# Second MLP: product 3 behind product 2, an earlier activation split, other places for the input splits, and a last quarter turned by TensorE

## The chip, the cores and the metric

The kernel runs on one core of a Trainium2 chip. The metric is the device time of one execution in microseconds; the kernel before takes 965.82 us (median of 3 runs, 965.8 to 967.69). A smaller number is better.

## The reference

The reference chains three blocks in float32. Attention: 4 x 8 heads, 576 positions, 64 channels, with a causal mask and a forgetting bias. Then two MLPs over 2304 tokens of width 512 with 2048 hidden units:

```python
x = np.ascontiguousarray(attn_out.transpose(0, 2, 1, 3)).reshape(B * S, H * D)
h = x @ w_in;  g = np.maximum(h, 0.0) + alpha * np.minimum(h, 0.0);  x = g @ w_out     # first MLP
h = x @ w_in;  r = np.maximum(h, 0.0);  g = r * r;                   out = g @ w_out   # second MLP
```

The weights come as float64 and are converted on the chip.

## The kernel before

**Precision.** A float32 operand is split into a rounded part and the rest (`split2`: ScalarE copies into the rounded type, VectorE subtracts, L927 and L928). A matmul of two such operands takes three terms (`TERMS`).

**Order.** Attention comes first, then the first MLP, then the second. The first MLP runs 48 steps: 3 passes of 768 tokens by 16 blocks of hidden units. A step is 24 matmuls into two `ph` banks (L601), the activation on VectorE (`gg`, L621 and L622), its split `gs` (L624, L625), and 24 matmuls into `po` (L887) for the step before. Beside it, weights are converted from float64 (`conv`: two ScalarE, two VectorE and one GpSimd instruction; L120 to L129). `convert(step, behind)` takes from the list `todo` what is due at that step, and `issue_after(behind)` puts it behind a given instruction on that instruction's engine. At steps 3 to 11 two conversions are due at each; they are all written ahead of the step's matmuls.

**Second MLP.** It uses a seven-product scheme (Strassen's, in Winograd's form) on halves: for each of 3 passes of 768 tokens, stage 1 makes the hidden activations and stage 2 the output.

- Stage 1 loops over 8 blocks q. Each has seven products of 6 matmuls of 384 columns (L1012), into four PSUM banks: a (products 1 and 2), b (6 and 7), c (5 and 3), d (4). The order on TensorE is 1, 6, 5 of block q, then product 3 of block q-1 (`end(q - 1)`), then 2, 4, 7 of block q. ScalarE copies a to `p1` behind product 1 (L1031), before product 2 accumulates into a. Behind product 7, VectorE makes u3 = p1 + b (L1060) and c22 = u3 + c (L1061). c22 reads bank c, into which product 3 then accumulates; so product 3 of a block waits for c22 of that block. `end` then adds c to u2 (L1043), and ScalarE and GpSimd square the activation (L1022, L1023). For odd q VectorE also subtracts two slots of `g` (L1047).
- The weights of stage 1 arrive in groups of up to 512 columns (`w1f`) and are split into `w1h` by `split2`, fetched three groups ahead.
- Stage 2 has 28 items (i, q): seven products by four quarters, in `ORDER2`, each a block of 12 matmuls (L1144), first the six of output half m = 0, then the six of m = 1. Its operand `th` (3 buffers) is a split of `g`, written by `prepare` `AHEAD` = 2 items ahead; for products 6, 7 and 4 a subtraction of two slots of `g` comes first (L1095).
- In `fill(n)`, behind block n of stage 2, the eleven steps of the next pass's input split (`x_steps`: splits into `xc` and differences in `xl`) are spread over the blocks n in (2, 3, 4, 5, 6, 7, 13, 14, 24, 25, 26), each behind the latest `th` split on ScalarE and VectorE.
- At the end of an output quarter VectorE adds the accumulator to `k` (L1164) and turns it in 32 x 32 blocks (L1130), and four DMAs store it with 256-byte rows (`store`, L1108). The last quarter of the last pass ends the kernel.

**What sets the order.** In the second MLP `in_order` chains TensorE's instructions as written. On the other engines a planner sets the order: it lays the program out on simulated time and takes, among the instructions that are ready, the one written first. `chain` still holds the last TensorE instruction of the pass before when a pass starts.

Of the kernel before, what the change touches and what calls it, by code (L numbers as in the profile page):

```python
# [8 lines left out]
F32 = mybir.dt.float32  # L9
# [10 lines left out]
def attention_then_two_mlps(  # L20
# [13 lines left out]
    nc = tc.nc  # L34
    B, H, S, D = q.shape
    P = 128
# [964 lines left out]
    def stage1(stream, fill):  # L1001

        def product(i, q, pt, first, last):
            s = SLOT[i]
            hl = stream.need(q, s // 2)
            c0 = (s % 2) * 256
            cnt = 0
            for kb in range(2):  # L1010
                for a, b in TERMS:
                    nc.tensor.matmul(  # L1012
                        pt[:, :HT], hl[:, a, c0 + kb * P : c0 + (kb + 1) * P], xc[i][:, b, kb, :],
                        start=(first and cnt == 0), stop=(cnt == 5), skip_group_check=not first,
                    )
                    cnt += 1

        def t15(name):
            return pools["m2"].tile([P, HT], F32, name=name, tag=name, bufs=2)

        def act(dst, r, h):
            nc.scalar.activation(r, h, AF.Relu)  # L1022
            nc.gpsimd.tensor_tensor(dst, r, r, ALU.mult)  # L1023

        hold = {}

        def begin(q):
            a, b, c, d = bank("a"), bank("b"), bank("c"), bank("d")
            product(1, q, a, True, True)
            p1 = t15("p1")  # L1030
            nc.scalar.copy(p1, a[:, :HT])  # L1031
            product(6, q, b, True, True)
            u2 = t15("u2")
            nc.vector.tensor_add(u2, p1, b[:, :HT])
            if q % 2 == 0:
                g_t[q // 2] = pools["m2"].tile([P, 2, 4, HT], F32, name="g", tag="g", bufs=NQ // 2)
            g = g_t[q // 2][:, q % 2]
            hold[q] = a, b, c, d, p1, u2, g

        def end(q):  # L1040
            a, b, c, d, p1, u2, g = hold.pop(q)
            product(3, q, c, False, True)
            nc.vector.tensor_add(u2, u2, c[:, :HT])  # L1043
            act(g[:, 1, :], u2, u2)
            if q % 2:
                gq = g_t[q // 2]
                last_g[0] = ins_of(nc.vector.tensor_sub(gq[:, :, 1], gq[:, :, 1], gq[:, :, 0]))  # L1047

        for q in range(NQ):
            begin(q)  # L1050
            a, b, c, d, p1, u2, g = hold[q]
            product(5, q, c, True, True)
            if q > 0:
                end(q - 1)
            product(2, q, a, False, True)
            act(g[:, 0, :], g[:, 0, :], a[:, :HT])
            product(4, q, d, True, True)
            product(7, q, b, False, True)
            u3, c22 = t15("u3"), t15("c22")
            nc.vector.tensor_add(u3, p1, b[:, :HT])  # L1060
            nc.vector.tensor_add(c22, u3, c[:, :HT])  # L1061
            nc.vector.tensor_add(u3, u3, d[:, :HT])
            act(g[:, 3, :], c22, c22)
            act(g[:, 2, :], u3, u3)
            fill(NQ - 1 - q)
            in_order(IN_ORDER[:1])
        return lambda: end(NQ - 1)

    PLACE = {1: 0, 5: 1, 6: 1, 2: 2, 7: 0, 4: 2, 3: 3}
    ORDER2 = (1, 5, 6, 2, 7, 4, 3)  # L1070
    AHEAD = 2

    class Stage2:


        def __init__(self, p):
            self.p = p
            self.items = [(i, q) for i in ORDER2 for q in range(NQ // 2)]
            self.th, self.slab, self.done, self.subs = {}, {}, 0, []

# [20 lines left out]
        def store(self, mh, h, yt):  # L1101
            for u in range(4):
                cs = slice(mh * 256 + 64 * u, mh * 256 + 64 * (u + 1))
                src = yt[32 * u : 32 * (u + 1)].rearrange("r j c m -> r j (c m)")
                e = nc.scalar if (self.p, mh, h) == (1, 0, 1) and u % 2 else nc.sync
                if self.p < 2:
                    r0 = (2 * self.p + h) * S
                    e.dma_start(out[r0 : r0 + HT, cs].rearrange("(j r) c -> r j c", r=32), src)  # L1108
                    continue
                for z in range(2):  # L1110
                    r0 = (2 * h + z) * S + 3 * P
                    e.dma_start(
                        out[r0 : r0 + 3 * TAIL, cs].rearrange("(j r) c -> r j c", r=32), src[:, 6 * z : 6 * (z + 1)]
                    )

        def run(self, fill):
            kept = {}
# [11 lines left out]
            def turn(yt, src, m):  # L1129
                nc.vector.transpose(yt[:, :, :, m], src)  # L1130

            accs = {}
            for n, (i, q) in enumerate(self.items):
                self.prepare(n + AHEAD)

# [3 lines left out]
                acc = accs[j]  # L1139
                th = self.th.pop((i, q))  # L1140
                ws = self.slab[i, q // 2]
                for m, qq, z in [(m, qq, z) for m in range(2) for qq in range(2) for z in range(3)]:
                    x, y = TERMS[z]
                    nc.tensor.matmul(  # L1144
                        acc[m][:, :HT], ws[:, y, (2 * q + qq) % 4, m * P : (m + 1) * P], th[:, x, qq, :],
                        start=(i == j and q == 0 and qq == 0 and z == 0),
                        stop=(q == NQ // 2 - 1 and qq == 1 and z == 2), skip_group_check=True,
                    )
                fill(n)
                if q < NQ // 2 - 1:  # L1150
                    continue
# [25 lines left out]
    handed = 0  # L1177
    xl_now[0] = xT[0]

    def convert(step, behind):  # L1180
        while todo and todo[0][0] <= step:
            with tc.issue_after(behind):
                _, what, args = todo.pop(0)
                what(*args)
            if loads and what in (w_conv, prep_conv):
                w_load(*loads.pop(0))

    for step, (c, f) in enumerate(steps):
        wi_now = wi
        if step >= 3:  # L1190
            convert(step, anchor)
        if step > 0 and step + 1 < len(steps):
            wi = split_w(0, steps[step + 1][1], 0)
        if step >= 3:
# [13 lines left out]
        pend.append([c, f, gs, wo])  # L1208
        if len(pend) > 1:
            mlp_out(*pend.pop(0))  # L1210
        if step < 3:
            convert(step, last_gg[0])
            in_order((mybir.EngineType.DVE, mybir.EngineType.Activation))
# [23 lines left out]
    pools["m2"] = ctx.enter_context(tc.tile_pool(name="m2", bufs=1, reuse_waits="tile"))  # L1237
    pools["ps"] = ctx.enter_context(tc.tile_pool(name="ps", bufs=8, space=PSUM, reuse_waits="tile"))

    PASSES = (0, 2, 1)  # L1240
    for z, p in enumerate(PASSES):
        s2 = Stage2(p)

        def early(left):
            with tc.issue_after(last_w1[0]):
                if left < 4:
                    i, q = s2.items[2 * (3 - left)]
                    s2.fetch(i, q // 2)
                if left == NQ // 2 and z + 1 < NPASS:
                    load_x(PASSES[z + 1])  # L1250
            if left == 0:
                s2.prepare(AHEAD)

        chain["at"] = len(nc.cur_bb.bb.instructions)
        close = stage1(stream if z == 0 else Stream(), early)
        steps2 = x_steps() if z + 1 < NPASS else []

        def fill(n):
            if n == 1:
                close()  # L1260
            in_order(IN_ORDER[:1])
            if n in (2,3,4,5,6,7,13,14,24,25,26) and steps2:
                with tc.issue_after(s2.last[0]), tc.issue_after(s2.last[1]):
                    steps2.pop(0)()

# [32 lines left out]
```

## Time and profile before

| | |
|---|---|
| median of 3 runs | 965.82 us |
| profiled execution, own time | 965.55 us |
| its span, first to last instruction | 963.8 us |
| outside the span | 1.75 us |
| TensorE busy (matmuls) | 946.8 us, 98% |
| VectorE busy | 787.7 us, 82% |
| ScalarE busy | 552.0 us, 57% |
| GpSimd busy | 340.1 us, 35% |
| granted TensorE clock, mean | 0.996 |

The profile has several views. The page gives the busy time of each engine. The view by windows gives busy time and number of instructions of each engine in chosen stretches. The view of waits lists how long an engine sat idle and what ended the idle time. The timeline lists the instructions of a stretch in order of time, merged where one line repeats: start, duration, engine, line, operation, tiles (written <- read), shape, count, and in brackets idle time and what ended it. The view of one line or tile gives durations as least/median/most. PE is TensorE, DVE VectorE, ACT ScalarE, POOL GpSimd, SP SyncE; a q behind a name is that engine's queue issuing DMAs. A matmul's duration overlaps the next one's, so the distance between starts is its price.

### The profile page before, as it was taken

What the parts mean: (1) busy time and instruction counts of PE and PEld (TensorE: products, weight loads), DVE (VectorE), ACT (ScalarE), POOL (GpSimd) and SP (SyncE); (2) the same over time, 40 slices, a digit from 0 to 9 for tenths busy, and PEclk for the clock granted to TensorE, in tenths of its full rate; (3) what the DMA queues carried; (4) which work ended last, traced back from release to release, by engine and by line L of the source; (5) the groups of instructions that cost most, each with busy time, mean ns of one, the idle gap of its engine ahead of it and who ended that gap; (6) DMA issues with size and microseconds to landing.
All of it is one profiled execution on the core that took longest, in us unless ns stands there. A gap on an engine that the chain in (4) does not pass through costs nothing.

```text
span 963.8 us, 16690 instructions
## 1 busy us (share of the span) xinstructions
PE 946.8 (98%) x5951; PEld 891.3 (92%) x5951; DVE 787.7 (82%) x1423; ACT 552.0 (57%) x1146; POOL 340.1 (35%) x341
## 2 busy tenths in 40 slices
PE   8999999999999999999999999999999999999997
PEld 6888888898999999999999999999999999999997
DVE  7788878879888887778987868788987899878685
ACT  6899888846544543345644634566435664366432
POOL 7466554133333453453253410343004430044200
PEclk9999999999999999999999999999999999999999
DMA  5777765324444344434653632676756767547385
GB/s 142 197 201 200 185 163 130 85 92 135 131 131 132 109 159 142 142 127 159 214 173 120 197 120 74 198 273 204 254 150 182 279 193 260 140 128 268 121 257 127
DMA packets 121446, 161.33 MB, mean 167 GB/s; under 512 B 50546, under 2 KB 94706, under 8 KB 115986
## 3 DMA queue, kind: packets, MB, share of 16 engines
q1 hardware_dynamic: 120112, 159.69, 54.1%
q8 instruction: 47, 0.77, 0.3%
q10 hardware_dynamic: 1250, 0.57, 0.3%
q14 instruction: 37, 0.30, 0.1%
HBM read 121.85 MB, written 30.11 MB: 158 GB/s over the span
## 4 chain that ended last, share of the span: by engine, by line
PE 84%; DVE 8%; issue 2%; ACT 2%; DMA 2%; SPq 1%; POOL 0%; ACTq 0%; DVEq 0%; POOLq 0%
PE ph L601 18%; PE po L887 17%; PE acc L1144 15%; PE ps_tr L500 5%; PE c L1012 4%; PE a L1012 4%; PE b L1012 4%; PE ps_xb L550 3%; PE d L1012 2%; PE ps_xa L534 2%; PE ps_sc L392 2%; PE ps_sc L393 2%; PE ps_tr L321 2%; PE ps_sc L398 2%; DVE xc L928 1%
## 5 line engine op out<-in xcount | busy, mean ns | idle before, releaser
L601 PE MATMUL ph<-xs,wi_hi 128*128 128x384 f32 x768 | 195.7, 335 | 1.2 <-DVE gg L622 1.2
L1144 PE MATMUL acc<-th,w2s 128*128 128x384 f32 x1008 | 176.7, 335 | 0.5 <-DVE th L928 0.5
L1144 PEld LDWEIGHTS acc<-th,w2s 128*128 128x128 f32 x1008 | 174.8, 188 | 1.5 <-DVE th L928 1.5
L887 PE MATMUL po<-gs,wo_hi 128*128 128x256 f32 (+1 forms) x768 | 166.1, 336 | 0.0
L601 PEld LDWEIGHTS ph<-xs,wi_hi 128*128 128x128 f32 x768 | 136.0, 188 | 3.6 <-DVE gg L622 1.5
L887 PEld LDWEIGHTS po<-gs,wo_hi 128*128 128x128 f32 x768 | 121.3, 188 | 14.0
L601 PE MATMUL ph<-xs,wi_lo 128*128 128x384 f32 x384 | 128.3, 334 | 0.0
L927 ACT CAST th<-g 128x768 fp32r<-128x768 f32 x84 | 70.3, 837 | 74.7 <-PE acc L1144 61.1
L624 ACT CAST gs<-gg 128x768 fp32r<-128x768 f32 (+1 forms) x48 | 39.8, 829 | 113.3 <-DVE gg L622 113.2
L928 DVE TENSOR_TENSOR w1h<-w1f,w1h 128x512 fp32r<-128x512 f32 x96 | 79.1, 825 | 29.8 <-ACT w1h L927 29.7
L887 PE MATMUL po<-gs,wo_lo 128*128 128x256 f32 (+1 forms) x384 | 98.9, 335 | 0.0
L928 DVE TENSOR_TENSOR th<-g,th 128x768 fp32r<-128x768 f32 x84 | 83.2, 990 | 17.1 <-ACT th L927 16.6
L129 POOL TENSOR_TENSOR wf<-cv_t,wf 128x512 uint32<-128x512 uint32 x32 | 45.8, 1430 | 92.7 <-DVE cv_t L125 78.0
L129 POOL TENSOR_TENSOR wc<-cv_t,wc 128x512 uint32<-128x512 uint32 x24 | 39.4, 1646 | 104.6 <-DVE cv_t L125 52.4
L625 DVE TENSOR_TENSOR gs<-gg,gs 128x768 fp32r<-128x768 f32 (+1 forms) x48 | 46.6, 971 | 36.3 <-ACT gs L624 36.3
L1023 POOL TENSOR_TENSOR g<-g 128x384 f32<-128x384 f32 x24 | 19.9, 829 | 155.7 <-ACT g L1022 155.7
L621 DVE TENSOR_SCALAR gg<-ph,alpha_sb 128x384 f32<-128x384 f32 x95 | 58.0, 611 | 19.9 <-PE ph L601 19.9
L419 DVE CUSTOM_DVE_ANT_0 pr<-ps_sc,mask 128x128 f32<-128x128 f32 (+3 forms) x128 | 61.7, 486 | 15.1 <-PE ps_sc L393 12.1
L601 PEld LDWEIGHTS ph<-xs,wi_lo 128*128 128x128 f32 x384 | 72.0, 188 | 0.1
L927 ACT CAST w1h<-w1f 128x512 fp32r<-128x512 f32 x96 | 53.8, 564 | 31.8 <-PE b L1012 8.2
L432 ACT ACTIVATE pr<-pr,nmax 128x128 f32<-128x128 f32 (+3 forms) x128 | 71.2, 557 | 0.4
L887 PEld LDWEIGHTS po<-gs,wo_lo 128*128 128x128 f32 x384 | 59.3, 188 | 7.7
(167 smaller groups left out, 2022.9 us busy)
## 6 DMA issues: line engine op xcount, KB each, us to landing
w2s<-w2D SPq DMA_DIRECT2D x42, 1024.0 KB
w1f<-w1D SPq DMA_DIRECT2D x72, 256.0 KB
raw_w<-in_moe_w_in_dram SPq DMA_DIRECT2D x32, 512.0 KB
w2D<-whl SPq DMA_DIRECT2D x16, 896.0 KB
raw_w<-in_moe_w_out_dram SPq DMA_DIRECT2D x24, 512.0 KB
iv<-sD SPq DMA_DIRECT2D x32, 144.0 KB
raw_q<-in_q_dram SPq DMA_DIRECT2D x16, 256.0 KB
raw_v<-in_v_dram SPq DMA_DIRECT2D x32, 128.0 KB
```

Of the source, the lines that this page charges most:

```text
L129: nc.gpsimd.tensor_tensor(d, tt, d, ALU.add)
L419: nc.vector.tensor_tensor_reduce(o, banks.pop(("s", i, h))[:, :w], m, -1.0, first, ALU.add, ALU.min, nmax[:, h : h + 1])
L432: nc.scalar.activation(o, o, AF.Exp, bias=m, scale=-1.0, accum_out=sums_of[n][:, i, h : h + 1])
L500: last = nc.tensor.transpose(ps[:, z * P : (z + 1) * P], pr[:, c0 : c0 + P], ident)
L601: nc.tensor.matmul(ph[h][:, :HT], ws[a][:, kb * P : (kb + 1) * P], xs[kb][:, bb, h * HT : (h + 1) * HT], start=(cnt == 0), stop=(cnt == 3 ...
L621: nc.vector.tensor_scalar(x, ph[h][:, :HT], 0.0, alpha_sb[:, f : f + 1], ALU.min, ALU.mult)
L625: sub = nc.vector.tensor_sub(z[:, 1], a, z[:, 0].bitcast(F32))
L887: nc.tensor.matmul(acc, ws[a][:, m * P : (m + 1) * P], gs[:, bb, c_], start=first_ and z == 0, stop=lst and z == 2, skip_group_check=True,)
L927: a = nc.scalar.copy(dst[:, 0], src)
L928: v = nc.vector.tensor_sub(dst[:, 1], src, dst[:, 0].bitcast(F32))
L1012: nc.tensor.matmul(pt[:, :HT], hl[:, a, c0 + kb * P : c0 + (kb + 1) * P], xc[i][:, b, kb, :], start=(first and cnt == 0), stop=(cnt == 5), ...
L1144: nc.tensor.matmul(acc[m][:, :HT], ws[:, y, (2 * q + qq) % 4, m * P : (m + 1) * P], th[:, x, qq, :], start=(i == j and q == 0 and qq == 0 ...
```

## The change

Six edits, all but one in the second MLP:

1. In stage 1, product 2 and the activation of its result are written ahead of `end(q - 1)`, so product 3 of the block before follows product 2.
2. `AHEAD` is 3, and stage 2's first three `th` are prepared one block of stage 1 earlier (`left == 1`).
3. The input split of the next pass goes to the blocks (2, 3, 4, 5, 12, 13, 14, 24, 25, 26, 27).
4. `chain.clear()` at the start of a pass: TensorE's first instruction of a pass is no longer chained to the last one of the pass before.
5. In the last pass the last quarter of the output is done by `finish`. TensorE's order is block n (m = 0), block n-1 (m = 1), three turns of m = 0, block n (m = 1), three turns of m = 1. VectorE adds m = 1 in three parts of 128 columns, TensorE turns each against the identity into PSUM, ScalarE or VectorE copies it out, and three DMAs of 128 rows of 1 KB store it, two on SP's queue and one on ScalarE's.
6. In the first MLP at steps 3 to 11, one conversion is written ahead of the step and the rest behind `mlp_out`, with VectorE's part behind the step's `gg`.

```diff
             product(5, q, c, True, True)
+            product(2, q, a, False, True)
+            act(g[:, 0, :], g[:, 0, :], a[:, :HT])
             if q > 0:
                 end(q - 1)
-            product(2, q, a, False, True)
-            act(g[:, 0, :], g[:, 0, :], a[:, :HT])
             product(4, q, d, True, True)
...
-    AHEAD = 2
+    PASSES = (0, 2, 1)
+    AHEAD = 3
...
+        def finish(self, n, block, acc, k2):
+            y = pools["m2"].tile([P, 3, P, 2], F32, name="yt", tag="yt", bufs=2)
+            tp = [bank(f"t{tb}") for tb in range(3)]
+
+            def add(m, c):
+                nc.vector.tensor_add(k2[:, m, c], k2[:, m, c], acc[m][:, c])
+
+            def turn(m, tb):
+                nc.tensor.transpose(tp[tb][:, m * P : (m + 1) * P], k2[:, m, tb * P : (tb + 1) * P], ident)
+
+            def evac(m, tb, e):
+                (nc.scalar.copy if e else nc.vector.tensor_copy)(y[:, tb, :, m], tp[tb][:, m * P : (m + 1) * P])
+
+            block(n, 0)
+            add(0, slice(0, HT))
+            block(n - 1, 1)
+            for tb in range(3):
+                turn(0, tb)
+            for tb in range(3):
+                evac(0, tb, 1)
+            block(n, 1)
+            for tb in range(3):
+                add(1, slice(tb * P, (tb + 1) * P))
+            for tb in range(3):
+                turn(1, tb)
+                evac(1, tb, tb < 2)
+                r0 = (2 * self.p + 1) * S + tb * P
+                (nc.scalar if tb == 1 else nc.sync).dma_start(
+                    out[r0 : r0 + P, 0:256], y[:, tb].rearrange("p f m -> p (f m)")
+                )
+            in_order(IN_ORDER[:1])
...
-                for m, qq, z in [(m, qq, z) for m in range(2) for qq in range(2) for z in range(3)]:
+                if not self.final or n < len(self.items) - 2:
+                    block(n, 0)
+                    block(n, 1)
+                elif n < len(self.items) - 1:
+                    block(n, 0)
+                else:
+                    self.finish(n, block, acc, kept[2])
+                    return
...
-    def convert(step, behind):
-        while todo and todo[0][0] <= step:
+    def convert(step, behind, n=99):
+        while todo and todo[0][0] <= step and n > 0:
+            n -= 1
...
-            convert(step, anchor)
+            convert(step, anchor, 1 if step < 12 else 99)
...
             mlp_out(*pend.pop(0))
+        if 3 <= step < 12:
+            convert(step, last_gg[0])
...
-            if left == 0:
+            if left == 1:
                 s2.prepare(AHEAD)

+        chain.clear()
         chain["at"] = len(nc.cur_bb.bb.instructions)
...
-            if n in (2,3,4,5,6,7,13,14,24,25,26) and steps2:
+            if n in (2,3,4,5,12,13,14,24,25,26,27) and steps2:
```

## Rows read from the trace of the kernel before

**Rows 1.** Page, part 1: busy us (share of the span), number of instructions.

```profile
PE 946.8 (98%) x5951; PEld 891.3 (92%) x5951; DVE 787.7 (82%) x1423; ACT 552.0 (57%) x1146; POOL 340.1 (35%) x341
```

**Rows 2.** By windows, stages 1, then stages 2: busy (count) PE, PEld, DVE, ACT, POOL.

```profile
599.40:660.00 60.60, 58.22 (x333) 57.06 (x331) 48.32 (x76) 35.56 (x72) 25.89 (x29) 1.00 0.70 237
720.00:779.30 59.30, 57.86 (x332) 57.09 (x331) 47.45 (x75) 35.17 (x70) 26.43 (x29) 1.00 0.67 213
839.40:898.40 59.00, 57.86 (x332) 57.10 (x331) 45.49 (x72) 33.57 (x67) 26.50 (x29) 1.00 0.54 168
660.00:720.00 60.00, 59.75 (x343) 59.23 (x343) 55.02 (x72) 29.27 (x39) 3.87 (x4) 1.00 0.68 210
779.30:839.40 60.10, 59.88 (x345) 59.36 (x344) 55.13 (x72) 29.26 (x39) 3.90 (x4) 1.00 0.65 208
898.40:957.90 59.50, 59.49 (x343) 59.17 (x341) 44.45 (x58) 23.29 (x30) 2.44 (x3) 1.00 0.65 197
```

**Rows 3.** Waits of TensorE over the span: us, times, longest.

```profile
PE c L1012 <- DVE c L1061: 5.0, 8, 1.0
...
PE acc L1144 <- DVE th L928: 0.5, 2, 0.2
```

**Rows 4.** Timeline, TensorE, stage 1 of the second pass.

```profile
755.56 1.20 PE L1012 MATMUL a<-xc,w1h 128*128 128x384 f32 x6
...
757.64 1.21 PE L1012 MATMUL c<-xc,w1h 128*128 128x384 f32 x6
759.85 1.28 PE L1012 MATMUL c<-xc,w1h 128*128 128x384 f32 x6 [1.01 <-DVE c L1061]
```

**Rows 5.** Timeline, VectorE, the same stretch.

```profile
753.96 0.54 DVE L1043 TENSOR_TENSOR u<-u,c 128x384 f32<-128x384 f32 x1
...
755.98 1.32 DVE L928 TENSOR_TENSOR w1h<-w1f,w1h 128x512 fp32r<-128x512 f32 x1 [1.15 <-ACT w1h L927]
757.23 0.94 DVE L1047 TENSOR_TENSOR g<-g 128x768 f32<-128x768 f32 x1
758.10 0.54 DVE L1060 TENSOR_TENSOR u<-p,b 128x384 f32<-128x384 f32 x1
...
759.16 0.54 DVE L1061 TENSOR_TENSOR c<-u,c 128x384 f32<-128x384 f32 x1
```

**Rows 6.** Timeline, ScalarE and GpSimd, the same stretch.

```profile
756.79 0.48 ACT L1031 COPY p<-a 128x384 f32<-128x384 f32 x1 [0.33 <-PE a L1012]
...
755.93 0.83 POOL L1023 TENSOR_TENSOR g<-g 128x384 f32<-128x384 f32 x1
```

**Rows 7.** Timeline, TensorE and ScalarE, start of the first pass.

```profile
599.43 1.21 PE L1012 MATMUL a<-xc,w1h 128*128 128x384 f32 x6
...
601.69 0.48 ACT L1031 COPY p<-a 128x384 f32<-128x384 f32 x1
```

**Rows 8.** Timeline, VectorE, stage 2 of the second pass.

```profile
799.07 0.95 DVE L928 TENSOR_TENSOR th<-g,th 128x768 fp32r<-128x768 f32 x1
```

**Rows 9.** Timeline, VectorE and TensorE, first MLP, step 5.

```profile
236.88 1.77 DVE L125 SCALAR_TENSOR_TENSOR cv_t<-cv_g,cv_t 128x512 uint32<-128x512 uint32 x1
...
239.18 0.62 PE L601 MATMUL ph<-xs,wi_hi 128*128 128x384 f32 x2 [1.16 <-DVE gg L622]
```

**Rows 10.** Timeline, all engines, end of the kernel.

```profile
956.52 1.38 PE L1144 MATMUL acc<-th,w2s 128*128 128x384 f32 x7
...
958.53 0.58 DVE L1130 STREAM_TRANSPOSE yt<-k 128x384 f32<-128x384 f32 x1
959.13 0.83 SPq L1108 DMA_DIRECT2D out_dram<-yt  x2
```

**Rows 11.** DMA, 957 to 964 us: GB/s in 40 slices of 0.175 us.

```profile
GB/s 0 0 0 0 0 0 0 0 0 0 0 0 0 0 0 0 6 136 155 157 155 151 142 104 130 259 256 217 226 147 9 0 0 0 0 0 0 0 0 0
```

**Rows 12.** Views of lines 500 and 359: ns least/median/most, first and last start.

```profile
L500 PE MATMUL ps_tr<-ident,pr x320: 270/272/332, 18.0 to 194.0; 128*128 128x128 f32 x160
...
L359 ACT CAST KS<-ps_tr x16: 247/252/266, 11.9 to 176.4; 128x128 fp32r<-128x128 f32 x16
```

More of the change, by code (lines that the diff above doesn't have):

```diff
@@ L1070, in attention_then_two_mlps @@
     ORDER2 = (1, 5, 6, 2, 7, 4, 3)
-    AHEAD = 2
+    PASSES = (0, 2, 1)
+    AHEAD = 3
     class Stage2:
         def __init__(self, p):
-            self.p = p
+            self.p, self.final = p, p == PASSES[-1]
             self.items = [(i, q) for i in ORDER2 for q in range(NQ // 2)]
@@ L1104, in store @@
                 src = yt[32 * u : 32 * (u + 1)].rearrange("r j c m -> r j (c m)")
-                e = nc.scalar if (self.p, mh, h) == (1, 0, 1) and u % 2 else nc.sync
+                e = nc.sync
                 if self.p < 2:
@@ L1130, in turn, with block @@
                 nc.vector.transpose(yt[:, :, :, m], src)
-            accs = {}
+            accs, ops = {}, {}
+            def block(n, m):
+                fresh, q, acc, th, ws = ops[n]
+                for qq, z in [(qq, z) for qq in range(2) for z in range(3)]:
+                    x, y = TERMS[z]
+                    nc.tensor.matmul(
+                        acc[m][:, :HT], ws[:, y, (2 * q + qq) % 4, m * P : (m + 1) * P], th[:, x, qq, :],
+                        start=(fresh and q == 0 and qq == 0 and z == 0),
+                        stop=(q == NQ // 2 - 1 and qq == 1 and z == 2), skip_group_check=True,
+                    )
             for n, (i, q) in enumerate(self.items):
@@ L1141, in run @@
                 ws = self.slab[i, q // 2]
-                for m, qq, z in [(m, qq, z) for m in range(2) for qq in range(2) for z in range(3)]:
[L1143 to L1148, printed above, removed]
+                ops[n] = i == j, q, acc, th, ws
+                if not self.final or n < len(self.items) - 2:
[6 more added lines that the diff above has]
+                    return
                 fill(n)
@@ L1238, in attention_then_two_mlps @@
     pools["ps"] = ctx.enter_context(tc.tile_pool(name="ps", bufs=8, space=PSUM, reuse_waits="tile"))
-    PASSES = (0, 2, 1)
     for z, p in enumerate(PASSES):
```

## Prediction

> **What bounds the kernel now.** I read the page first. TensorE is busy for 98% of the span, VectorE for 82% [rows 1]. So only two kinds of time can be had: moments in which TensorE waits, and the end, after its last matmul. The matmuls stay as many, apart from six small turns. The windows by stage, read second, say where TensorE loses time. The product that starts at 755.56 and the one at 757.64, with one product between, put a product at 1.04 us [rows 4]. A stage 1 window holds 55 products, 57.2 us, but the three windows are 60.6, 59.3 and 59.0 us long: 3.4 + 2.1 + 1.8 = 7.3 us lost. A stage 2 window holds 28 blocks of two products and the last product 3, 59.3 us, against 60.0, 60.1 and 59.5: 0.7 + 0.8 + 0.2 = 1.7 us [rows 2]. The waits, read third, name the cause. In stage 1 product 3 waits for c22 on VectorE, 8 times, 1.0 us at most; in stage 2 a block waits twice for its `th` [rows 3]. The idle times listed are smaller than the losses because a restart refills the pipe and gaps that are short aren't listed.
>
> **Product 3 behind product 2.** The longest wait: product 3 could have started at 757.64 + 1.04 = 758.68 and started at 759.85, 1.17 us late [rows 4]. c22 began at 759.16 and took 0.54, so the matmul followed 0.15 us behind its end [rows 5]. The change puts one more product, 1.04 us, between c22's release and product 3. If c22 stays where it is, this worst case is 0.13 us late and all the others, shorter, vanish. That alone gives back nearly all of the 7.3 us.
>
> Does c22 stay? VectorE's order ahead of it is a weight split at 755.98, the subtraction L1047, u3, one more weight split, c22 [rows 5]. The weight split waited for ScalarE, whose queue held the activations. L1047 needs the square of product 3's result, so product 3's delay could pass through L1047 to c22, and then nothing would be gained. The rows speak against it. L1043, the add that follows product 3, ran at 753.96 [rows 5], while product 3 of that block ended near 755.56 - 3 x 1.04 = 752.44 plus some 0.2 us of pipe. It was 1.3 us late because VectorE was busy, not for want of product 3. A delay of 1.04 us fits in that. GpSimd's last square before L1047 is of product 2's result, at 755.93 [rows 6]; product 2 now comes earlier, which takes that square out of the way.
>
> Every instruction that moves: product 2's six matmuls, one ScalarE activation and one GpSimd square go a product earlier; product 3's six matmuls, L1043, its activation, its square and L1047 a product later, and the weight fetch that `product` triggers follows them on SP's queue, ScalarE and VectorE. It is needed four products or more later. Product 2 now has two products, 2.08 us, instead of three for ScalarE's copy of bank a. That copy ends 756.79 + 0.48 - (755.56 + 1.04) = 0.67 us behind product 1 in the pass shown [rows 4, 6], and at worst 601.69 + 0.48 - (599.43 + 1.04) = 1.70 us [rows 7]. With 0.15 us to the matmul both fit. Since the planner lays out VectorE anew, I leave 0.7 us of loss: gain 6.6 us, bounds 0 and 7.3.
>
> GpSimd's squares matter in another way. The weight split at 755.98 is 1.32 us long, and the square of 0.83 us runs beside it from 755.93 on [rows 5, 6]; if they shut each other out, a square that moves can lengthen another split by up to its own 0.8 us. The Trainium skill, SBUF — State Buffer, section "Who interferes with whom", says just this: a VectorE instruction with two SBUF inputs and a GpSimd instruction that reads SBUF block each other for a whole instruction. In the sum I take it that the number of such meetings ahead of c22 doesn't grow; that it does is a rival below.
>
> **Stage 2.** The lost 0.7 and 0.8 us lie in the two passes that also split the next input; the third, which doesn't, loses 0.2. VectorE is busy 55 of 60 us there, against 44 in the third pass [rows 2]. The `th` splits come late behind the input steps: the one at 799.07 ends at 800.02, just as its block starts. A step is one such instruction of 0.95 us [rows 8]. The change takes two steps, 1.9 us, out of the crowded blocks 6 and 7 and puts one each at 12 and 27, and `AHEAD` = 3 puts the steps 2 to 5 behind one more `th`. Three buffers still let a `th` be written only when the block three before is done, so `AHEAD` alone shortens nothing. What is late next: blocks 16 to 23, where a subtraction and a split, 1.9 us, meet a block of 2.08 us, and one more step comes ahead of them. I expect small waits there, 0.1 to 0.4 us a pass. Gain 1.1 us, bounds -0.5 and 1.6. Clearing the chain lets the planner place the next pass's first products early where it sees TensorE idle; their operands are split long before, and I cost it at nothing.
>
> **First MLP.** One wait: 1.16 us plus the refill, 1.4 us, for `gg`, held up on VectorE by a conversion of 1.77 us [rows 9]. With one of two conversions behind `gg` this should shrink, but the same conversions remain, and the one moved comes ahead of the split of `gs`, which has a whole product group of cover. Taken at half, 0.7 us; bounds -0.5 and 1.4.
>
> **The end.** The last matmul starts 1.38 - 0.33 = 1.04 us behind 956.52 and ends at 957.90; VectorE's last turn ends at 959.11, the store is issued at 959.13 [rows 10], data flow from 959.8 to 962.4 [rows 11], and the span ends at 963.8, 1.4 us later. After the change: three turns of m = 0 precede the last half block. Line 500 has 272 ns for such a turn [rows 12], which overlaps the next one; a third of a 384-column matmul's distance (1.04 / 6 = 0.17 us [rows 4]) would be 0.06. I take 0.11 apiece, nearer to that, since the matmuls' own durations are twice their distance, so the last matmul ends at 958.2. They wait for VectorE's add of 0.5 us, covered by block n-1's half, 1.04 us; without that cover the block behind would wait 0.5 us. Then the first add of 128 columns (between 0.54 / 3 and 0.54, taken 0.3), a turn (0.3), a copy (0.25 [rows 12]) with about 0.1 us of signals: first store issued at 959.3, second and third 0.2 us apart, 959.7 with the issue of two on one queue. Data of the last start 0.7 us behind its issue, as now, at 960.4. 131 KB at the rates of [rows 11], 150 to 260 GB/s, take 0.5 to 0.9 us: end of data near 961.2 instead of 962.4, so 1.2 us gained; bounds 0.3 and 1.9.
>
> Whether a turn costs 0.11 or 0.27 us decides 0.5 us of this; the end of the range is kept below. Here a page speaks against the change: the Trainium skill, VectorE: DVE Perf Modes, section "The three transpose paths", has 390 ns for a 128 x 128 turn on TensorE and 311 ns on VectorE. By its figure the three turns ahead of the last half block would cost 1.2 us, an estimate from that page, and the end would gain 0.3 us instead of 1.2; the 272 ns of line 500 [rows 12] don't agree with it.
>
> **The sum.** 965.55 - 6.6 - 1.1 - 0.7 - 1.2 = 955.95 us in the profiled execution's terms. It lies 0.27 us below the median, so 956.2.
>
> **The rivals.**
> - *c22 moves along with product 3.* The planner puts L1047 or another weight split ahead of u3 so that c22 comes later by most of a product. For it: L1047 already stands there [rows 5]. Against: the slack of L1043. Half of stage 1's gain is lost: 959.5; all of it: 962.8. Chance 0.14.
> - *The moved squares hit the splits ahead of c22.* For it: the one meeting shown [rows 5, 6]. Against: it is there already, and the square of product 2 moves away from it. One more hit of 0.8 us at each of the 8 waits leaves each only 1.04 - 0.8 = 0.24 us shorter, 1.9 us gained in stage 1 instead of 6.6: 960.9. Chance 0.06.
> - *Turns aren't pipelined.* At 0.27 us each the three ahead of the last half block cost 0.8 instead of 0.3 us: 956.7. Chance 0.08, inside the forecast's own range.
> - *The change doesn't bring stage 1 and 2 what it says.* VectorE's new layout makes waits at other products as long as those removed; the end and the first MLP alone give 963.9. Chance 0.1.
> - *Slower: product 2 waits for the copy of a.* The place is ScalarE's queue ahead of L1031; the copy would have to end later than 1.9 us behind product 1. It ends at 0.67 us mostly. Four more ScalarE instructions as long as the copy, 0.48 us [rows 6], ahead of it in each block make 2.59, 0.69 us too late; 24 blocks, 16.6 us, more than the 9.6 gained: 972.8. It decides from 0.4 us a block. Chance 0.06.
>
> **How the numbers follow.** The forecast, 956.2, gets 0.56, with the turns' rival 0.64; with the terms' bounds its own range is 953.6 to 959. The range takes in the rivals on c22 and the squares: 954.0 to 962.8, leaving out the slower rival, the one on waits elsewhere and the very best case. A measurement of this kernel tells 0.2%, 1.9 us, from no change. Faster: the forecast and the rivals on c22, squares and turns, 0.84, and half of the one on waits elsewhere, whose 963.9 lies at that bound: 0.89; same 0.05; slower 0.06.
>
> **What would show it.** In the waits, product 3 behind c22 gone or under 0.3 us in all; stage 1 windows near 57.5 us, stage 2 near 59.6; in the first MLP no wait for `gg`; in the timeline of the end, the last store issued 1.5 us behind the last matmul's end (958.2 to 959.7 above) and its data done 1.5 us after that. Wrong would be a new wait of product 2 for `p`, of blocks 16 to 23 for `th`, or c22 as late against product 3 as before.

## The result and the profile after

The changed kernel takes 955.3 us (median of 4 runs, 954.66 to 955.52) against 965.81 us (964.74 to 967.69) of the kernel before, run beside it: a ratio of 0.9888, 95% interval 0.9871 to 0.9905. The forecast was 956.2. The profiled execution took 954.66 us, with a span of 952.9; that is 10.9 us less than the profiled execution before.

The page, part 1, of the changed kernel (as [rows 1]), and after it the six stages of the second MLP by windows (as [rows 2], here in order of time: stage 1, stage 2, and so on; columns: busy time and count of TensorE, its weight loads, VectorE, ScalarE, GpSimd; granted clock; DMA share; GB/s):

```profile
PE 944.1 (99%) x5957; PEld 891.8 (94%) x5957; DVE 781.6 (82%) x1424; ACT 554.4 (58%) x1151; POOL 342.4 (36%) x341
```

```profile
597.90:655.15 57.25, 57.25 (x333) 57.25 (x332) 43.81 (x75) 34.84 (x72) 24.00 (x28) 1.00 0.74 248
655.15:718.70 63.55, 63.55 (x367) 63.55 (x367) 57.89 (x76) 31.56 (x44) 6.53 (x6) 1.00 0.63 203
718.70:771.80 53.10, 53.10 (x309) 53.10 (x307) 44.29 (x72) 34.08 (x66) 26.30 (x28) 1.00 0.72 235
771.80:835.35 63.55, 63.55 (x367) 63.55 (x367) 57.18 (x75) 31.35 (x43) 4.80 (x5) 1.00 0.64 202
835.35:888.45 53.10, 53.10 (x308) 53.10 (x307) 41.85 (x69) 32.31 (x63) 25.73 (x28) 1.00 0.56 181
888.45:948.20 59.75, 59.75 (x346) 59.51 (x345) 44.02 (x57) 23.87 (x33) 2.64 (x4) 1.00 0.63 196
```

Compare the length of each window with its busy time. Before, the stage 1 windows were 1.1 to 2.4 us longer than TensorE was busy [rows 2]; now the two are equal in every window. (Stage 2 of the first two passes holds 24 more matmuls than before and the next stage 1 holds 24 fewer: with the chain cleared, four products of the next pass stand among its blocks.) TensorE never waits in the second MLP until its end.

The waits of TensorE over the span (as [rows 3]; columns: us in total, times, longest), all of them:

```profile
PE ps_xa L657 <- DVE warm L663: 2.2, 1, 2.2
PE ps_tr L321 <- POOL hl_k L311: 0.9, 1, 0.9
PE ps_sc L392 <- DVE nmax L419: 0.7, 1, 0.7
PE ps_sc L393 <- DMA KH<-cumD: 0.5, 1, 0.5
PE t L1125 <- DVE k L1122: 0.5, 1, 0.5
PE ps_tr L500 <- ACT KH L288: 0.2, 1, 0.2
PE po L887 <- DVE gs L625: 0.2, 1, 0.2
PE ps_sc L393 <- ACT KH L687: 0.2, 1, 0.2
```

Product 3's eight waits for c22, 5.0 us, are gone, and so are those for `th` [rows 3] and for `gg` [rows 9]. The one wait in the second MLP (`t`, L1125) is the end's: TensorE waits for VectorE's first 128-column add, with nothing else to do.

**Where the 10.9 us came from.** The distance from one matmul's start to the next, less the usual 0.174 us of a 384-column matmul (1.04 / 6, [rows 4]), summed over a stage where it is more than 0.03 us, gives what the stage lost. Behind the last matmul the count starts at the end of its 0.174 us. Summed so:

| | lost before, us | lost after, us | gained, us | forecast, us |
|---|---|---|---|---|
| stage 1, three passes | 3.34 + 2.05 + 1.76 = 7.15 | 0 | 7.15 | 6.6 |
| stage 2, three passes | 0.67 + 0.64 + 0 = 1.31 | 0 | 1.31 | 1.1 |
| first MLP | 1.43 | 0.46 | 0.97 | 0.7 |
| last matmul to the span's end | 6.03 | 4.71 + 0.35 for the turns ahead | 0.97 | 1.2 |

That is 10.4 us. The other 0.5 us is attention, which the change doesn't touch: the second MLP's first product starts 1.49 us earlier, of which the first MLP explains 0.97. It counts as the difference between two executions: over the fourteen profiles of this case the first MLP starts anywhere from 195.5 to 196.4 us, in the one before at 196.31 and in the one after at 195.81.

### The profile page after: what moved, and what is told of

Its sections match the earlier page's. It is cut to its first block, busy times and chain, and to the rows that moved or that the text cites. A ratio compares the mean times of both kernels' runs of the same rounds, so it can differ in the third digit from the quotient of the medians.

```text
span 952.9 us, 16715 instructions
## 1 busy us (share of the span) xinstructions
PE 944.1 (99%) x5957; PEld 891.8 (94%) x5957; DVE 781.6 (82%) x1424; ACT 554.4 (58%) x1151; POOL 342.4 (36%) x341
## 4 chain that ended last, share of the span: by engine, by line
PE 93%; DMA 2%; DVE 2%; SPq 1%; ACT 1%; issue 1%; POOL 0%; ACTq 0%; DVEq 0%; POOLq 0%
PE po L887 19%; PE ph L601 19%; PE acc L1171 18%; PE a L1012 5%; PE c L1012 5%; PE b L1012 5%; PE ps_tr L500 5%; PE ps_xb L550 3%; PE d L1012 3%; PE ps_xa L534 2%; PE ps_sc L392 2%; PE ps_sc L393 2%; PE ps_tr L321 2%; PE ps_sc L398 2%; DMA raw_w<-in_moe_w_in_dram 1%
## 5 line engine op out<-in xcount | busy, mean ns | idle before, releaser
L928 DVE TENSOR_TENSOR th<-g,th 128x768 fp32r<-128x768 f32 x84 | 80.1, 954 | 24.5 <-ACT th L927 24.3
L928 DVE TENSOR_TENSOR w1h<-w1f,w1h 128x512 fp32r<-128x512 f32 x96 | 74.1, 774 | 20.6 <-ACT w1h L927 19.9
L129 POOL TENSOR_TENSOR wf<-cv_t,wf 128x512 uint32<-128x512 uint32 x32 | 48.0, 1499 | 89.0 <-DVE cv_t L125 74.0
L1023 POOL TENSOR_TENSOR g<-g 128x384 f32<-128x384 f32 x24 | 23.6, 982 | 149.7 <-ACT g L1022 149.6
L625 DVE TENSOR_TENSOR gs<-gg,gs 128x768 fp32r<-128x768 f32 (+1 forms) x48 | 50.9, 1061 | 30.8 <-ACT gs L624 30.6
L576 ACT CAST wi_hi<-wf 128x512 fp32r<-128x512 f32 x46 | 28.7, 625 | 75.3 <-PE ph L601 72.2
```

What stands on the lines that cost most here:

```text
L129: nc.gpsimd.tensor_tensor(d, tt, d, ALU.add)
L625: sub = nc.vector.tensor_sub(z[:, 1], a, z[:, 0].bitcast(F32))
L928: v = nc.vector.tensor_sub(dst[:, 1], src, dst[:, 0].bitcast(F32))
```

## The experiments

Two questions were open. Does stage 1 gain because product 3 has one more product of cover, or because c22 itself comes earlier? And what is each of the other edits worth? Twelve kernels answer them. "c22 behind product 7" below is the time from the end of product 7's last matmul slot to the end of the add that writes c22 and lets product 3 into bank c, read from the timeline of all 24 blocks. In the old order three products, 3.12 us, lie between; in the new one four, 4.16 us. With the 0.15 us that the matmul follows c22's end by [rows 4, 5], c22 may be late by 2.97 us in the old order and 4.01 us in the new one.

Ratios are against the kernel before on the same chip. The last three columns are read from one profiled execution of each kernel.

| kernel | median, us | ratio, 95% interval | c22 at worst, us | 512-column weight splits over 1 us, of 72 | stage 1 lost, us |
|---|---|---|---|---|---|
| before | 965.81 | | 4.15 | 28 | 7.15 |
| changed kernel | 955.3 | 0.9871 to 0.9905 | 3.31 | 13 | 0 |
| order_alone | 957.86 | 0.9906 to 0.9936 | 3.44 | 14 | 0 |
| order_undone | 962.06 | 0.9951 to 0.9979 | 4.78 | 30 | 8.56 |
| cast_first | 958.79 | 0.9902 to 0.9935 | 3.29 | 13 | 0.55 |
| no_square2 | 960.32 | 0.9925 to 0.9962 | 3.42 | 10 | 1.25 |
| double_new | 959.45 | 0.9911 to 0.9945 | 4.42 | 3 | 1.05 |
| double_old | 972.97 | 1.0049 to 1.0088 | 4.29 | 1 | 14.55 |

**order_alone and order_undone.** The edit on the order, alone on the kernel before, and the change without it:

```diff
-            if q > 0:
-                end(q - 1)
             product(2, q, a, False, True)
             act(g[:, 0, :], g[:, 0, :], a[:, :HT])
+            if q > 0:
+                end(q - 1)
```

> The kernel before with edit 1 alone: product 2 ahead of product 3 of the block before. Theory S (slack): one more product, 1.04 us, between c22 and product 3 is what removes the waits; c22 stays about 4 us behind product 7 at worst. Then the three stage 1 windows are near 57.3 us each, waits of product 3 for c22 under 0.3 us in all, stage 2 still loses 0.7 and 0.8 us, and the time is 965.8 - 6.9 = 958.9. Theory L (layout): the planner's new order of VectorE, brought about by the other edits, is what made c22 early. Then this edit alone leaves c22 where it was or moves it later with product 3, and some 2 to 4 us of stage 1's loss remain: 960.5 to 962.8.

> The changed kernel with edit 1 alone taken back. Theory S: the waits of product 3 come back, 5 to 7 us in the three stages 1: 960.5 to 962.5. Theory L: in the second and third pass of the changed kernel c22 ends 2.1 to 2.6 us behind product 7, and the old order allows 2.97, so nothing is lost there; in the first pass up to 3.3 us, a loss of 0.3 us at each of four blocks: 956.5.

The edit alone gains 0.79% (ratio 0.9921), 7.7 us against the 965.56 us that the kernel before took beside it, and stage 1 loses nothing any more. Taken out of the change, it brings c22's wait back: the median is 6.8 us above that of the changed kernel. (The 8.56 us in the table are those of the profiled execution, which took 963.98 us, the longest of five; that the loss is larger than before isn't shown.) The waits of TensorE in the change without it:

```profile
PE c L1012 <- DVE c L1061: 6.3, 7, 1.6
```

So this edit carries most of the gain. But the column on c22 was a surprise: the forecast held that c22 stays where it is, and in order_alone its worst lateness fell from 4.15 to 3.44 us. The old order would have lost about 1.0 us with such a c22 (the sum over the blocks of what exceeds 2.97).

**cast_first and no_square2.** Both keep TensorE's old order, and ask what makes c22 late. The first writes product 3's activation a block later and places it behind the last weight cast on ScalarE; the second leaves out GpSimd's square of product 2's activation (that part of the hidden activation stays unsquared).

```diff
 def end(q):
     ...
     nc.vector.tensor_add(u2, u2, c[:, :HT])
-    act(g[:, 1, :], u2, u2)
+    def rest():
+        act(g[:, 1, :], u2, u2)
     ...
+def late():
+    with tc.issue_after(last_cast[0]):
+        rest[0]()
```

```diff
-            nc.gpsimd.tensor_tensor(dst, r, r, ALU.mult)
+            if square:
+                nc.gpsimd.tensor_tensor(dst, r, r, ALU.mult)
...
-            act(g[:, 0, :], g[:, 0, :], a[:, :HT])
+            act(g[:, 0, :], g[:, 0, :], a[:, :HT], False)
```

> The kernel before with TensorE's order kept (product 3 ahead of product 2), but the activation of product 3's result (ScalarE's activation, GpSimd's square, L1047) written a block later, behind the weight casts issued by then; u2 has three buffers instead of two. Theory Q (queue): in the kernel before, ScalarE's queue holds two weight casts behind an activation that waits for L1043, so a weight split comes on VectorE only after product 7 and pushes c22 back; edit 1 helped above all because it turned that order. Then c22 ends 2 to 3.3 us behind product 7 as in the run of edit 1 alone, and the waits of product 3 shrink from 7.2 us of loss to under 1.5 us: 959.5 to 960.5. Theory S (slack): the distance between c22 and product 3 on TensorE is what counts, and c22 comes early in the changed kernel only because TensorE no longer waits. Then the waits stay above 4 us: 963 or more.

> The kernel before without GpSimd's square of the activation of product 2 (24 instructions; the part of the output that hangs on it is not squared). Theory G: the meeting of this square with the weight split, 1.32 us against 0.68, is what makes c22 late. Then the long splits (over 1 us) fall from 28 of 72 to about 14, c22 comes 0.6 us earlier and the waits of product 3 fall from 5.0 to about 1.5 us. Theory Q: the split is late because of ScalarE's queue; without the square it is shorter by 0.6 us, but still starts behind product 7: c22 still 3.3 us or more behind product 7 where it was 4, a loss of 2 to 4 us in stage 1.

Without any change of TensorE's order, cast_first takes 6.6 of the 7.15 us away, and no_square2 takes 5.9. In no_square2 both activations still stand ahead of the two weight casts on ScalarE; besides the square that is missing, the planner moved one weight cast and its split ahead of c22 in nine blocks that had been early. VectorE's timeline of it, the block that answers to [rows 5] (columns: start, duration, line, tiles; line numbers are shifted by one):

```profile
752.24 0.69 DVE L928 TENSOR_TENSOR w1h<-w1f,w1h 128x512 fp32r<-128x512 f32 x1 [1.04 <-ACT w1h L927]
752.85 0.95 DVE L1048 TENSOR_TENSOR g<-g 128x768 f32<-128x768 f32 x1
753.71 0.55 DVE L1061 TENSOR_TENSOR u<-p,b 128x384 f32<-128x384 f32 x1
754.18 0.69 DVE L928 TENSOR_TENSOR w1h<-w1f,w1h 128x512 fp32r<-128x512 f32 x1
754.78 0.55 DVE L1062 TENSOR_TENSOR c<-u,c 128x384 f32<-128x384 f32 x1
```

The same split that took 1.32 us beside GpSimd's square [rows 5, 6] takes 0.69 us without it. So in the kernel before, that square is a cause of c22's lateness: it meets the weight split ahead of c22. The rule of the Trainium skill that the forecast weighed (SBUF — State Buffer, "Who interferes with whom") holds here, 1.32 against 0.69 us, but it worked for the change, not against it. In cast_first the casts run ahead of product 3's activation, and the squares stay as many. The split still meets parts of one or two squares there (0.79 to 0.97 us), but in 20 of the 24 blocks it starts 0.85 us ahead of product 7's end, where in the seven latest blocks of the kernel before it starts 0.1 to 0.4 us behind it. How much of the lateness is the meeting itself and how much the later start of the split, these two runs don't separate: the meeting shown is worth 0.63 us, and c22 came up to 1.6 us earlier in no_square2 and up to 1.9 in cast_first.

**double_new and double_old.** Since both causes were now at work, the cover was measured by itself. In order_alone and in cast_first, c22's add is written twice; the second add releases bank c. The orders differ, the lateness is made alike.

```diff
             nc.vector.tensor_add(c22, u3, c[:, :HT])
+            nc.vector.tensor_add(c22, u3, c[:, :HT])
```

> The kernel before with TensorE's new order alone (order_alone) and c22's add on VectorE written twice, so that the second one releases bank c about 0.5 us later. It asks how much cover the new order gives by itself. In order_alone c22 ended 3.44 us behind product 7's end at worst; from the rows of before, the old order allows about 2.97 us and the new one 4.0. Theory (the added product is 1.04 us of cover): c22's latest end moves to 3.8 to 4.1 us, stage 1 still loses under 0.8 us in all, 957.9 to 958.9 us. Rival (the new order helps only because c22 itself comes earlier in it): product 3 waits again at the eight blocks where c22 is latest, 0.5 us each and more, stage 1 loses 3 to 5 us, 961 to 963 us.

> The same doubled add of c22 in cast_first: TensorE's old order, product 3's activation behind the weight casts on ScalarE. There c22 ended 3.29 us behind product 7 at worst and stage 1 lost 0.55 us. Theory (the old order has no cover left): c22's latest end moves to 3.7 to 4.0 us, each of the eight to twelve late blocks loses another 0.5 us, stage 1 loses 4 to 7 us, 962.5 to 965 us. Rival (a late c22 costs the old order little, TensorE waited for something else in before): under 1.5 us lost in stage 1, 958.8 to 960 us.

The second add moved c22 further than the 0.5 us expected, since the planner put a weight split between the two. VectorE in double_old, in a block of the second pass:

```profile
745.01 0.55 DVE L1072 TENSOR_TENSOR c<-u,c 128x384 f32<-128x384 f32 x1
745.48 0.69 DVE L928 TENSOR_TENSOR w1h<-w1f,w1h 128x512 fp32r<-128x512 f32 x1
746.08 0.55 DVE L1034 TENSOR_TENSOR u<-p,b 128x384 f32<-128x384 f32 x1
746.54 0.55 DVE L1073 TENSOR_TENSOR c<-u,c 128x384 f32<-128x384 f32 x1
```

and TensorE in the same block, where product 3 starts 0.15 us behind that second add's end (747.09):

```profile
745.38 1.21 PE L1012 MATMUL c<-xc,w1h 128*128 128x384 f32 x6
747.24 1.30 PE L1012 MATMUL c<-xc,w1h 128*128 128x384 f32 x6 [0.65 <-DVE c L1073]
```

With that, c22 was 1.9 to 4.3 us late in double_old and 1.9 to 4.4 us in double_new, 3.3 to 3.8 us late in 18 and 13 of the 24 blocks. What exceeds 2.97 us sums to 13.2 us in the one and 11.0 in the other: nearly the same c22. The waits of TensorE for it, first in double_old, then in double_new:

```profile
PE c L1012 <- DVE c L1073: 10.0, 19, 1.2
```

```profile
PE c L1012 <- DVE c L1062: 0.2, 1, 0.2
```

Nineteen waits against one; 14.55 us lost in stage 1 against 1.05; 972.97 us against 959.45. The two limits account for the sizes. The 13.2 us beyond 2.97 stand against the 14.55 lost in double_old; what exceeds 4.01 gives 1.0 us in double_new. The same sum over the kernel before gives 6.5 by 2.97 (7.15 were lost) and 0.2 by 4.01. So had c22 stayed as late as before, the new order alone would have given nearly everything back. The forecast's mechanism is real; what it did not see is that a second one, sufficient too, came with it. double_old's expected time, 962.5 to 965 us, was missed by 8 us, because c22 moved by 1.5 us in 13 of the 24 blocks and by 0.6 to 1.2 us in the others, and not by 0.5. double_new came out above its range too (957.9 to 958.9), since c22 was up to 4.42 us late and not 4.1 at most.

**places_undone and ahead_undone.** The change with the input splits in the old blocks, and the change with the activation splits two blocks ahead as before:

```diff
-            if n in (2,3,4,5,12,13,14,24,25,26,27) and steps2:
+            if n in (2,3,4,5,6,7,13,14,24,25,26) and steps2:
```

```diff
-    AHEAD = 3
+    AHEAD = 2
...
-            if left == 1:
+            if left == 0:
```

> The changed kernel with the steps of the input split in the old blocks (2 to 7, 13, 14, 24 to 26); AHEAD stays 3. If the places are what removed stage 2's waits, the 0.7 and 0.6 us come back in the two passes: 956.6. If AHEAD does it, the time stays at 955.3.

> The changed kernel with AHEAD = 2 and the first th prepared at the end of stage 1 as before; the new places stay. If the places do it alone, as the prediction has it, the time stays at 955.3 within 0.4 us and stage 2 loses under 0.4 us a pass. If AHEAD is needed, 0.6 us a pass come back: 956.5.

places_undone took 956.61 us (ratio 0.9895, 0.9875 to 0.9915), 1.3 us above the changed kernel, and as much above ahead_undone on the same chip; its stage 2 lost 0.58 us in each of the first two passes. TensorE waits twice for `th`, as in [rows 3]:

```profile
PE acc L1171 <- DVE th L928: 0.6, 2, 0.3
```

ahead_undone took 955.27 us (0.9881, 0.9862 to 0.9901) with no wait for `th`; the tightest `th` was written 0.23 us before its block. The places bring stage 2's gain, the earlier split nothing that can be measured.

**clear_undone, lean.** The change without `chain.clear()`, and without both the clearing and the third block ahead:

```diff
-        chain.clear()
         chain["at"] = len(nc.cur_bb.bb.instructions)
```

> The changed kernel with the chain kept from pass to pass. The four products that the changed kernel runs inside stage 2 of the pass before go back to the start of their own stage 1. If the hoisting is worth nothing, as the prediction has it, the time is 955.3 within 0.5 us and stage 2's blocks 16 to 23 wait for th by under 0.4 us a pass. If the hoisted products are what covers those blocks, 1 to 2 us come back: 956.5 to 957.5. If they are also what made c22 early in passes 2 and 3 (theory L's cause), c22 there ends 3 to 4 us behind product 7 again, with no wait as long as edit 1 stands.

> The change without the cleared chain and with the th splits two blocks ahead as before, both left out together. Each alone left the time where it was. Theory (both bring nothing, also together): 955.3 us within 0.5, no wait for th in stage 2. Rival (the four products hoisted into stage 2 take the place of time that a th then lacks, so that the two stand in for each other): th waits of 0.2 to 0.8 us in stage 2, 955.8 to 957 us.

The two kernels took 955.01 us (0.9892, 0.9872 to 0.9911) and 955.15 us (0.9887, 0.9871 to 0.9903). The second MLP of clear_undone is as long as that of the changed kernel, 350.1 against 350.2 us from its first product to its last matmul. lean has no wait for `th` either. In its first pass c22 came 4.54 us late once, which by the limit of 4.01 costs 0.53; stage 1 lost 0.59. Whether that comes of leaving out the two edits, one profile doesn't tell; the median shows no loss. So the four products that the cleared chain lets into stage 2 only change places, and by the medians the two edits can be left out.

**end_undone and conv_undone.** The change with the old end, and with the first MLP's conversions where they were:

```diff
-                e = nc.sync
+                e = nc.scalar if (self.p, mh, h) == (1, 0, 1) and u % 2 else nc.sync
...
-                if not self.final or n < len(self.items) - 2:
+                if True:
```

```diff
-            convert(step, anchor, 1 if step < 12 else 99)
+            convert(step, anchor)
...
-        if 3 <= step < 12:
-            convert(step, last_gg[0])
```

> The changed kernel with the end as before (VectorE's turns, four stores of 256-byte rows). The prediction's term: 1.2 us more, 956.5. From the two traces I read 1.32 us between last matmul and end of span, less 0.4 us for the three turns ahead of the last half block: 0.9 us more, 956.2. If the turns by TensorE bring nothing: 955.3.

> The change with the first MLP's input conversions as in the kernel before (both of a step ahead of gg). Theory: the wait for gg of 1.16 us is back, the first MLP loses 1.4 us; 0.5 to 1.0 us above the change's 955.3: 955.8 to 956.3 us. Rival (the conversions' place is worth nothing, since the other kernels that have the new place lose 0.9 us there as well): within 0.3 us of 955.3 us.

end_undone took 955.93 us (0.9901, 0.9881 to 0.9921). In the profiled executions its stretch behind the last matmul is 6.03 us again against 4.71, with 0.35 us of turns on the other side: the end is worth 0.97 us. The medians are 0.6 us apart, but the runs overlap (955.46 and 956.39 against 954.66 to 955.52), so they don't confirm it by themselves. conv_undone took 955.66 us (0.9892, 0.9876 to 0.9909) and has the wait for `gg` of 1.2 us back:

```profile
PE ph L601 <- DVE gg L622: 1.2, 1, 1.2
```

Its first MLP loses 1.42 us, as before. With the new place six profiled executions lost 0.87 to 0.94 us there, and only that of the changed kernel 0.46. So this edit is worth about 0.5 us, the profile shown above being a lucky one by another 0.4 us; the medians (0.36 us apart, between what the two theories expected) don't tell it from nothing.

## Why the forecast came out, point by point

**The sum.** For the profiled execution the forecast was 955.95 us; it took 954.66. The four terms brought 10.4 us instead of 9.6, and the attention 0.5 us that no term named, which is luck. So is about 0.4 us of the first MLP's term. The upper end of the forecast's own range, 959, doesn't follow from the terms' bounds: their lower ends add up to a loss of 0.7 us, 966.5.

**Product 3 behind product 2** (6.6 forecast, 7.15 measured). The waits are gone as foreseen, and the cover of one product is what the forecast said it is: double_new and double_old show it at the same lateness. The step that failed is "c22 stays where it is". It came earlier, in the late blocks by up to 2.1 us; in blocks that had been early it came later, by up to 1.4 us, but stayed within the new limit. Compare [rows 4 to 6] with the same block after. TensorE first: product 3 (the second `c`) now follows product 2, without a wait.

```profile
745.80 1.20 PE L1012 MATMUL a<-xc,w1h 128*128 128x384 f32 x6
746.84 1.20 PE L1012 MATMUL c<-xc,w1h 128*128 128x384 f32 x6
...
753.08 1.20 PE L1012 MATMUL a<-xc,w1h 128*128 128x384 f32 x6
```

VectorE, the block's weight split, u3, the subtraction, c22:

```profile
748.86 0.85 DVE L928 TENSOR_TENSOR w1h<-w1f,w1h 128x512 fp32r<-128x512 f32 x1
750.16 0.55 DVE L1060 TENSOR_TENSOR u<-p,b 128x384 f32<-128x384 f32 x1 [0.45 <-PE b L1012]
750.63 0.95 DVE L1047 TENSOR_TENSOR g<-g 128x768 f32<-128x768 f32 x1
751.50 0.55 DVE L1061 TENSOR_TENSOR c<-u,c 128x384 f32<-128x384 f32 x1
```

Before, one more weight split stood between u3 and c22 in this block; now it follows c22, at 751.96.

```profile
758.56 0.68 DVE L928 TENSOR_TENSOR w1h<-w1f,w1h 128x512 fp32r<-128x512 f32 x1
```

ScalarE and GpSimd ahead of it: product 2's activation, two weight casts, and only then product 3's activation; the square of product 2's result (`g<-g`) starts 0.71 us ahead of the split instead of with it.

```profile
747.04 0.49 ACT L1022 ACTIVATE g<-a 128x384 f32<-128x384 f32 x1 [0.18 <-PE a L1012]
747.42 0.40 ACT L927 CAST w1h<-w1f 128x256 fp32r<-128x256 f32 x1
748.12 0.62 ACT L927 CAST w1h<-w1f 128x512 fp32r<-128x512 f32 x1 [0.30 <-ACT w1h L927]
748.97 0.53 ACT L1022 ACTIVATE u<-u 128x384 f32<-128x384 f32 x1 [0.22 <-DVE u L1043]
```

```profile
748.15 1.00 POOL L1023 TENSOR_TENSOR g<-g 128x384 f32<-128x384 f32 x1
```

In this block u3 now waits for TensorE's product 7 and not for VectorE's queue. It starts 0.20 us behind the end of product 7 instead of 2.54 us, and c22 starts 1.34 us behind u3 instead of 1.06 us, since L1047 now stands between them and the weight split no longer does: 2.06 us earlier in all. c22 ends at 752.05, two products ahead of product 3, which comes behind the `a` of 753.08. Before, the casts stood behind both activations on ScalarE, as its timeline in the block of [rows 5] shows, and the first activation waited 1.45 us for VectorE's L1043:

```profile
754.54 0.53 ACT L1022 ACTIVATE u<-u 128x384 f32<-128x384 f32 x1 [1.45 <-DVE u L1043]
754.97 0.47 ACT L1022 ACTIVATE g<-a 128x384 f32<-128x384 f32 x1
755.34 1.13 ACT L927 CAST w1h<-w1f 128x512 fp32r<-128x512 f32 x2
```

Moving product 3 a product later took its activation out of their way. The forecast counted the moved activations and squares, but as a danger to be bounded, not as a gain.

**The rivals on c22.** "c22 moves along" named L1047 or a split ahead of u3; here L1047 went behind u3, and c22 came earlier. "The moved squares hit the splits" had the right mechanism, of which [rows 5, 6] show one meeting, and the wrong sign: splits over 1 us fell from 28 to 13. The forecast had itself noted that product 2's square gets out of the way, and left it out of the sum.

**The slower rival**, product 2 waiting for the copy of bank a, did not come: the copy ended 1.70 us behind product 1 at worst, the value read from [rows 7], under the 1.9 it has.

**Stage 2** (1.1 forecast, 1.31 measured). The forecast read 1.7 us of loss off the lengths of the windows, where the distances between matmuls give 1.31, with none in the third pass. That the places do it and `AHEAD` by itself does nothing was right. The small waits expected in blocks 16 to 23 did not come. That the cleared chain is worth nothing was right too.

**First MLP** (0.7 forecast, 0.97 in the two profiles, about 0.5 by the other executions). The wait for `gg` went as foreseen, but a wait for `gs` of 0.2 us stands in its place: the split that the forecast gave a whole product group of cover comes too late. Taking half of the 1.4 us was a guess, and came near.

**The end** (1.2 forecast, 0.97 measured). The timeline of the changed kernel's end, all engines but the weight loads:

```profile
946.76 0.49 PE L1125 MATMUL t<-ident,k 128*128 128x128 f32 x3
947.01 1.31 PE L1171 MATMUL acc<-th,w2s 128*128 128x384 f32 x6
...
948.35 0.68 DVE L1122 TENSOR_TENSOR k<-k,acc 128x128 f32<-128x128 f32 x3 [1.88 <-PE acc L1171]
...
948.79 0.69 PE L1125 MATMUL t<-ident,k 128*128 128x128 f32 x3 [0.47 <-DVE k L1122]
949.13 0.47 ACT L1128 COPY yt<-t 128x128 f32<-128x128 f32 x2 [1.45 <-PE t L1125]
949.43 0.83 SPq L1144 DMA_DIRECT2D out_dram<-yt  x2
949.52 0.29 DVE L1128 COPY yt<-t 128x128 f32<-128x128 f32 x1 [0.48 <-PE t L1125]
949.62 0.36 ACTq L1144 DMA_DIRECT2D out_dram<-yt  x1
```

The last matmul ends at 948.32. The first store is issued 1.11 us behind it (forecast 1.1), the last 1.56 us (forecast 1.5). Both came out, though the terms that the forecast lists up to the first store add up to only 0.95 us. The three turns ahead of the last half block take 0.49 us together and start 0.11 us apart, the value chosen. The Trainium skill (VectorE: DVE Perf Modes, "The three transpose paths") has 390 ns for a turn of 128 x 128 on TensorE, in bf16. The six turns here are float32 and took 270 to 300 ns each; the three ahead of the last half block cost 0.35 us together, against the 1.2 us estimated from that figure. Behind the last matmul the turns start 0.20 us apart, which is the pace of VectorE's three adds ahead of them. The data end 3.3 us behind the last matmul instead of 3.0, and that covers the 0.2 us which the term lacks:

```profile
GB/s 0 0 0 0 0 0 0 0 0 0 0 0 0 0 0 0 0 0 0 0 0 0 0 0 135 345 340 363 316 351 334 65 0 0 0 0 0 0 0 0
```

These are the DMA rates in 40 slices of 0.175 us from 946 us on. The three stores move together from 950.2 to 951.6, at up to 363 GB/s, against 104 to 259 before [rows 11]: faster, but the first of them, issued at 949.43, also starts only at 950.2, 0.8 us behind its issue, and the data of all three end together. The forecast had taken the last store, 131 KB, as the only one still to move; the slices add up to 393 KB, the bytes of all three.

## What to carry to other kernels

Where an engine waits for a result that passes through a queue of another one, first write down, for every block, how late the result is and how late it may be: the sum of the excess gave stage 1's loss here to within 10% where it was large (6.5 for 7.15, 13.2 for 14.55 us), whatever made the result late. An edit that moves one product on TensorE also moves its activation and its square on two other engines; ask of each whether it leaves a queue in which the result stood, since here that alone was worth as much as the cover. Edits that only give more room where there was room already (a third block ahead, a cleared chain) brought nothing.

## What the runs showed of the chip that was not expected

A weight split on VectorE of 128 x 512 takes 0.69 us alone and 1.32 us when GpSimd squares a 128 x 384 tile beside it [rows 5, 6]. In the trace of the kernel before, 45 of the 72 such splits start while a square runs. 42 of them end 0.55 us behind that square's end, wherever in it they start (the other three start in its last 0.12 us): one that starts 0.05 us into a square of 0.83 us takes 1.32 us, one that starts 0.46 us into it takes 0.91. So the split gets almost nowhere until the square is done. Taking away one of GpSimd's four squares a block made the kernel before 0.56% faster (ratio 0.9944), though GpSimd is busy for only 35% of the span [rows 1].

Data of stores with rows of 1 KB left at up to 363 GB/s; the old end's, with 256-byte rows, at up to 259 [rows 11]. The old end also had four stores and not three; no run separates the two.
